# Third output tiles of the last two halves as a Strassen pair, earlier scores for the last half, and packed masks

## The chip, the cores and the metric

One NeuronCore of a Trainium2 chip runs the whole kernel. The metric is device time in microseconds; the kernel before takes 241.64 us, the median of three runs (241.13 to 242.92).

Five engines work side by side, each with a queue of its own that it works off in order: PE (TensorE, matrix products), DVE (VectorE), ACT (ScalarE), POOL (GpSimd) and SP (which here only issues transfers). They wait for each other through semaphores. "PEld" in a profile is PE loading weights.

## The reference

```python
def _attn_ref(q, k, v, n_global, n_local):        # B, H, S, D = 4, 8, 768, 64
    scores = scale * np.matmul(q, k.transpose(0, 1, 3, 2))
    ...
    is_global = pos[None, :] < int(n_global)       # 8 first keys
    is_local = (rel >= 0) & (rel < int(n_local))   # the last 96 keys
    keep = is_global | is_local
    scores = np.where(keep, scores - slopes * dist, -1e9)
    ...                                            # softmax over keys
    return np.matmul(a, v)

def _moe_ref(x, w_gate, w_val, w_out):             # x: 3072 x 512, inner 1536
    gate = np.maximum(x @ w_gate, 0.0)
    val = x @ w_val
    return gate * val @ w_out
```

The output of the attention, with its 8 heads side by side, is the `x` of the gated network. Inputs and output are float32; the kernel multiplies in bfloat16.

## The kernel before

The 3072 rows are cut into eight *halves* (two per batch entry) of 384 rows, each of three tiles of 128 rows. For every half there are two jobs.

*Attention of a half*, cut into 26 small pieces by `attention_pieces`. Heads go in four pairs. For a pair, `pair_scores` makes the scores of two groups of key tiles in four PSUM banks (L397), `pair_exps` takes the exponential (L406, ACT), `masks` multiplies by a mask that holds the distance bias and the zeros (L359, DVE, one multiply per key tile; for odd halves three in the first group and two in the second, for even halves two and two). `piece_av` multiplies by the values (L427) and takes a logarithm (L436) and, once per pair, an exponential of its negative (L441) to get the reciprocal of the sums; `piece_norm` multiplies by it (L446, DVE) and so writes `xT`, the input of the network. The masks lie in `m_all`, made once by `make_mask` from the distances `dd`. Keys and queries of a later half are prepared by `early_pieces`: casts on POOL (L363), transposing transfers in SP's queue (L368), and copies of the keys into their tiles on POOL (`piece_order`, L259 to L265).

*The network of a half*, made by `ffn_pieces`. Twelve chunks of 128 inner columns: `gate` (four matmuls of 384 columns, L518, then a ReLU on ACT, L525) and `val` (four more, then a multiply on DVE that writes the chunk into `ht`, L531). Then the output. Of the three tiles of a half, the third is made plainly by `outp`: twelve matmuls of 512 columns (L538) in four parts, a copy on ACT (L543) and a store (L544). The first two are made together by Strassen's scheme for a 2 x 2 block product: seven products `p1` to `p7` of six matmuls of 256 columns (`block`, L583) in place of eight, with sums of parts of `ht` on the left (`sum_cb`, `sum_ad`, `sum_de`, DVE: L567, L571, L576), sums of parts of the output weights on the right (made once, L809), and additions and copies that put the results together (L599 to L629). Their stores are L593.

PSUM has eight banks: three (`ff`) for the network and five (`x`) for the attention and for the products `p2` and `p5`. The tiles of a pool are reused in turn, so that a new product waits until the one three (or five) before it has been read.

Half 0 and half 1 have a start of their own, and half 2's attention is worked into their end. From `c = 2` on, stage `c` is one turn of this loop, and sets the order of work: the network of half `c` is a list of items, each with a weight, and the pieces of the attention of half `c + 1` and of the preparation of half `c + 2` are laid over it.

```python
def spread(items, first, last):
    n = len(items)
    return [(first + (i + 0.5) / n * (last - first), f) for i, (_, f) in enumerate(items)]
```

`weave` issues the items of the network in order and adds up their weights; a piece is issued as soon as the sum has reached its place times the total weight. The order is fixed when the program is built: each engine's queue holds its instructions in the order in which they are issued here. In a stage the first item is the start of chunk 0 (weight 1.0), then its rest (0.15 and 0.15), then 22 items of 0.65 for the other chunks, then four parts of the third tile and seven products of 0.65 each.

Of the kernel before, what the change touches and what calls it, by code (L numbers as in the profile page):

```python
# [8 lines left out]
FP32 = mybir.dt.float32  # L9
BF16 = mybir.dt.bfloat16  # L10
AF = mybir.ActivationFunctionType
ALU = mybir.AluOpType
# [3 lines left out]
def kernel(  # L16
# [12 lines left out]
    nc = tc.nc  # L29

    B, H, S, D = q.shape
    NG = int(n_global)
    NL = int(n_local)
    DM = H * D
    DFF = moe_w_gate.shape[1]
    N_DC = DM // 128
    N_FC = DFF // 128
    HP = H // 2
    QH = S // 2
    NN = 3  # L40
    KT = 128 - NG
    PK = KT // NN
    WQ = 72
    NHALF = 2 * B
# [8 lines left out]
    for half in range(2):  # L53
        for j in range(NT):
            w0 = PK * j - 128 * half
            a, b_ = max(0, w0), min(128, w0 + WQ)
# [15 lines left out]
    late = {}  # L72
# [21 lines left out]
    wg = [const.tile([128, N_DC, GW * 128], BF16, name=f"wg{i}") for i in range(N_FC // GW)]  # L94
    wv = [const.tile([128, N_DC, GW * 128], BF16, name=f"wv{i}") for i in range(N_FC // GW)]
    wo_sb = const.tile([128, N_FC, DM], BF16)
    dd = const.tile([128, 2, NN, WQ], BF16)
    m_all = const.tile([128, H, 2, NN, WQ], BF16)

    def w_of(t, dc, fc):  # L100
# [70 lines left out]
    vb3 = firstp.tile([128, H, D], BF16, name="vb3")  # L171
    rc0 = [firstp.tile([128, QH], FP32, name=f"rc{p}") for p in range(HP)]
    kq0 = firstp.tile([128, 2, H, NN * D], FP32, name="kq0")
    kq1 = setupp.tile([128, 2, H, NN * D], BF16, name="kq1")

    def rows_of(src, s, h0, h1):
# [150 lines left out]
    def scores(s, p, g):  # L327
# [18 lines left out]
            c += NN * w  # L346
        nc.scalar.activation(es[:, :, 0:cols], ps[:, :, 0:cols], AF.Exp, bias=0.0, scale=scale)  # L347

    def masks(s, p, g, steps=steps_of):
        for j in steps[s % 2][g]:  # L350
            _, a, w, m = by[s % 2, j]
            es, c = es_of[s, p, j]
            for_all = es[:, :, c : c + NN * w]
            mk = m_all[:, 2 * p : 2 * p + 2, 0 if j == 0 else 1, :, m : m + w]
            if w == WQ:
                mk = mk.rearrange("k e n p -> k e (n p)")
            else:
                for_all = for_all.rearrange("k e (n p) -> k e n p", n=NN)
            nc.vector.tensor_mul(for_all, for_all, mk)  # L359
# [133 lines left out]
    def attention_pieces(s):  # L493
        QK = lambda p: [(0.15, lambda g=g: piece_qk(s, p, g)) for g in range(3)]
        AV = lambda p: [(0.29, lambda e=e: piece_av(s, p, e)) for e in range(2)]
        N = lambda p: [(0.0, lambda: piece_norm(s, p))]
        g = QK(3)
        a = AV(2)
        gap = [(0.0, lambda: None)]
        return (QK(0) + QK(1) + AV(0) + N(0) + gap + QK(2) + AV(1) + N(1) + gap  # L500
                + g[0:1] + a[0:1] + g[1:2] + a[1:2] + g[2:3] + N(2) + AV(3) + N(3))
# [4 lines left out]

    begin_of = {}

    def ffn_pieces(c):
        ht = ht_pool.tile([128, N_FC, QH], BF16, name="ht")  # L510
        st = {}
# [38 lines left out]
            if c == 2:  # L550
                product(wg, "g", 1, 0, N_DC - 1)


        N2, D2 = N_FC // 2, DM // 2
        tiles_ = [slice(n * 128, (n + 1) * 128) for n in range(2)]

        def sums_of(name, *shape):
            if name not in st:
                st[name] = late["sums"].tile([128, *shape], BF16, name=name)
            return st[name]  # L560

        cb = lambda: sums_of("cb", N2, 2, 128)
        ad = lambda: sums_of("ad", N2, 128)
        de = lambda: sums_of("de", N_FC, 128)

        def sum_cb(i0, i1):
            nc.vector.tensor_tensor(cb()[:, i0:i1].rearrange("f i n t -> f i (n t)"), ht[:, i0:i1, 0:256],  # L567
                                    ht[:, N2 + i0 : N2 + i1, 0:256], op=ALU.add)

        def sum_ad(i0, i1):  # L570
            nc.vector.tensor_tensor(ad()[:, i0:i1], ht[:, i0:i1, tiles_[0]],  # L571
                                    ht[:, N2 + i0 : N2 + i1, tiles_[1]], op=ALU.add)

        def sum_de(i0, i1):
            x, y = (1, 0) if i0 < N2 else (0, 1)
            nc.vector.tensor_tensor(de()[:, i0:i1], ht[:, i0:i1, tiles_[x]], ht[:, i0:i1, tiles_[y]],  # L576
                                    op=ALU.subtract)

        def block(key, pool, left, right, start, stop):
            if start:  # L580
                st[key] = psum[pool].tile([128, 512], FP32, name=f"{pool}_ps")
            for i in range(N2):
                nc.tensor.matmul(st[key][:, 0:D2], lhsT=left(i), rhs=right(i),  # L583
                                 start=start and i == 0, stop=stop and i == N2 - 1,
                                 skip_group_check=not start)
            return st[key][:, 0:D2]

        c0, c1 = slice(0, D2), slice(D2, DM)
        bs = lambda name: lambda i: late["bs"][name][:, i]
        V2 = nc.vector.tensor_tensor  # L590

        def store(n, cols, eng=nc.sync):
            eng.dma_start(out=out_v[c, n][:, cols], in_=st["r", n][:, cols])  # L593

        def p4():
            for n in range(2):
                st["r", n] = late["osb"].tile([128, DM], FP32, name="osb")
            ps = block("d", "ff", lambda i: ht[:, N2 + i, tiles_[1]], bs("b21-b11"), True, True)
            nc.scalar.copy(st["r", 0][:, c0], ps)  # L599

        def p3():
            ps = block("c", "ff", lambda i: ht[:, i, tiles_[0]], bs("b12-b22"), True, True)
            nc.scalar.copy(st["r", 0][:, c1], ps)

        def p1():
            ps = block("a", "ff", lambda i: ad()[:, i], bs("b11+b22"), True, True)
            nc.scalar.copy(st["r", 1][:, c1], ps)

        def p2():
            ps = block("b", "x", lambda i: cb()[:, i, 1], lambda i: wo_sb[:, i, c0], True, True)  # L610
            V2(st["r", 1][:, c0], ps, st["r", 0][:, c0], op=ALU.add)
            V2(st["r", 1][:, c1], st["r", 1][:, c1], ps, op=ALU.subtract)

        def p5():
            ps = block("e", "x", lambda i: cb()[:, i, 0], lambda i: wo_sb[:, N2 + i, c1], True, True)
            V2(st["r", 0][:, c1], ps, st["r", 0][:, c1], op=ALU.add)
            V2(st["r", 0][:, c0], st["r", 0][:, c0], ps, op=ALU.subtract)
            if c == NHALF - 1:
                store(1, c0)
                store(0, c1)  # L620

        def p6():
            ps = block("c", "ff", lambda i: de()[:, i], bs("b11+b12"), False, True)
            V2(st["r", 1][:, c1], ps, st["r", 1][:, c1], op=ALU.add)
            store(1, slice(0, DM) if c < NHALF - 1 else c1, nc.sync if c < NHALF - 1 else nc.scalar)

        def p7():
            ps = block("a", "ff", lambda i: de()[:, N2 + i], bs("b21+b22"), False, True)
            V2(st["r", 0][:, c0], ps, st["r", 0][:, c0], op=ALU.add)  # L629
            store(0, slice(0, DM) if c < NHALF - 1 else c0)  # L630

        behind = {2: [lambda: sum_de(0, 3)], 5: [lambda: sum_de(3, 6)], 8: [lambda: sum_cb(0, 3)],
                  9: [lambda: sum_ad(0, 3)], 10: [lambda: sum_de(6, 9)]}

        def val_and_sums(fc):
            val(fc)
# [5 lines left out]
        for fc in range(N_FC):  # L642
            f1.append((0.65, lambda fc=fc: gate(fc)))
            f1.append((0.65, lambda fc=fc: (val if c < 1 else val_and_sums)(fc)))
        f2 = [(0.65, lambda n=n, part=part: outp(n, part))
              for n in (range(NN) if c < 1 else (NN - 1,)) for part in range(4)]
        if c >= 2:
            f1[:2] = [(1.0, begin_of[c][0]), (0.15, begin_of[c][1]), (0.15, begin_of[c][2])]
        if c == 2:
            f1[0] = (1.5, f1[0][1])  # L650
            f1[3] = (0.15, lambda: gate(1, N_DC - 1))
        if c >= 1:
            f2 += [(0.65, f) for f in (p4, p3, p1, p2, p5, p6, p7)]
            for at, f in ((5, lambda: sum_de(9, 12)), (3, lambda: sum_cb(3, 6)), (2, lambda: sum_ad(3, 6))):
                f2.insert(at, (0.0, f))
        return f1, f2

# [1 line left out]
# [4 lines that stand above are left out]
# [119 lines left out]
    for f in ("m1 g0 m3 v0 m2 g1 K3 K2 m0 g3 K1 S30 S31 g2 K0 S20 v3 S11 v1 S21 A3 N3 v2 S00 S01 "  # L782
# [10 lines left out]
        else:  # L793
# [3 lines left out]
    early.close()  # L797
    ctx.enter_context(open_psum(ff=3, x=5))
    pool = ctx.enter_context(tc.tile_pool(name="late", bufs=1, reuse_waits="tile"))
    late["osb"] = ctx.enter_context(tc.tile_pool(name="osb", bufs=3, reuse_waits="tile"))  # L800
    late["sums"] = ctx.enter_context(tc.tile_pool(name="sums", bufs=1, reuse_waits="tile"))
    late["bs"] = {name: pool.tile([128, N_FC // 2, DM // 2], BF16, name=f"bs{i}")
                  for i, name in enumerate(("b21-b11", "b12-b22", "b11+b22", "b11+b12", "b21+b22"))}

# [14 lines left out]
    for f in (*casts[:7], lambda: nc.gpsimd.tensor_copy(held, wo_sb[0:1, N_FC - 1, 0:1]),  # L819
# [9 lines left out]
          [(0.33, order_k[2]), (0.38, order_k[3])],  # L829
          pieces, spread(early_pieces(3), 0.58, 0.88),  # L830
          spread([(0.0, lambda name=name, part=part: wo_sum(name, part)) for name in late["bs"] for part in range(2)],
                 0.1, 0.74))

    for c in range(2, NHALF):
        placed = []
        if c + 1 < NHALF:
            placed.append(spread(attention_pieces(c + 1), *((0.07, 0.82) if c == 2 else (0.0, 0.8))))
        if c + 2 < NHALF:
            load_qk(c + 2, 0, H)
            load_v_half(c + 2)  # L840
            placed.append(spread(early_pieces(c + 2), 0.25, 0.75))
        f1, f2 = ffn_pieces(c)
        weave(f1 + f2, *placed)

# [34 lines left out]
```

## Time and profile before

| | |
|---|---|
| runs | 242.92, 241.13, 241.64 us |
| profiled execution | 241.74 us, of which the span from first to last instruction is 239.9 |
| busy, share of the span | PE 97%, DVE 72%, ACT 64%, PEld 61%, POOL 36% |
| PE's granted clock | 0.998 of full speed |
| stage 5, 6, 7 begin at | 159.4, 186.4, 213.85 us |
| L518 (gate and val) | 768 matmuls, 80.7 + 80.2 us busy |
| L538 (plain output tiles) | 112 in the records, 29.6 us busy |
| L583 (Strassen products) | 294 matmuls |

"Busy" is the time in which an engine had an instruction under way. PE's matmuls overlap one another: a group's mean duration is longer than the spacing at which they follow each other, and the spacing is what adds up. The chain that ended last, followed in order of time, shows these spacings. A wait is the idle time of an engine ahead of an instruction, put down to the instruction that released it.

### The profile page before, as it was taken

How to read it: one execution, taken by the hardware profiler on the slowest of the kernel's cores; microseconds unless marked ns; L12 is line 12 of the kernel's file. 1: busy time of each engine (PE TensorE's matmuls, PEld its weight loads, DVE VectorE, ACT ScalarE, POOL GpSimd, SP SyncE). 2: the span in 40 equal slices, each digit the busy share in tenths (PEclk: the TensorE clock that was granted, in tenths of full speed). 3: DMA queues.
4: the chain of work that ended last, by engine and by line, in shares of the span. 5: the costliest groups of instructions: out<-in, count | busy, mean ns of one | idle time of the engine just before them, and what ended most of it. 6: DMA issues, size and time to landing. Idle time of an engine off the chain costs nothing.

```text
span 239.9 us, 5355 instructions
## 1 busy us (share of the span) xinstructions
PE 233.5 (97%) x1937; PEld 146.6 (61%) x1945; DVE 173.3 (72%) x456; ACT 153.4 (64%) x347; POOL 85.9 (36%) x202
## 2 busy tenths in 40 slices
PE   7899999999999999999999999999999999999994
PEld 3655555665458566666668566676658566676663
DVE  7775955869677788777787687866887677764643
ACT  5897883337775777748774777638774677733330
POOL 6767893208414860903274060902350000000000
PEclk9999999999999999999999999999999999999999
DMA  6999999993976997098519939398431200030003
GB/s 200 181 198 177 257 234 219 185 162 61 270 178 134 301 150 131 8 185 257 108 25 122 285 93 133 19 166 262 67 68 44 90 0 0 3 129 3 4 27 104
DMA packets 69603, 31.42 MB, mean 131 GB/s; under 512 B 47160, under 2 KB 66616, under 8 KB 69576
## 3 DMA queue, kind: packets, MB, share of 16 engines
q0 software_dynamic: 31744, 8.71, 35.3%
q1 hardware_dynamic: 36616, 21.45, 35.1%
q10 hardware_dynamic: 1216, 0.92, 1.2%
q8 instruction: 15, 0.25, 0.4%
q14 instruction: 12, 0.10, 0.1%
HBM read 28.41 MB, written 6.29 MB: 145 GB/s over the span
## 4 chain that ended last, share of the span: by engine, by line
PE 91%; ACT 3%; DVE 2%; issue 1%; ACTq 0%
PE ff_ps L518 53%; PE ff_ps L538 9%; PE ff_ps L583 8%; PE x_ps L427 6%; PE x_ps L397 4%; PE x_ps L583 3%; PE t_ps L459 2%; PE s_ps L341 2%; PE t_ps L272 1%; PE t_ps L682 1%; ACT lnd L436 1%; PE t_ps L310 1%; DVE xT L446 1%; PE s_ps L321 1%; ACT rcp L441 0%
## 5 line engine op out<-in xcount | busy, mean ns | idle before, releaser
L518 PE MATMUL ff_ps<-xT,wg 128*128 128x384 bf16 x384 | 80.7, 326 | 0.5 <-ACT grelu L525 0.4
L518 PE MATMUL ff_ps<-xT,wv 128*128 128x384 bf16 x384 | 80.2, 326 | 0.0
L531 DVE TENSOR_TENSOR ht<-ff_ps,grelu 128x384 bf16<-128x384 f32 x96 | 53.1, 554 | 28.5 <-PE ff_ps L518 13.8
L525 ACT ACTIVATE grelu<-ff_ps 128x384 bf16<-128x384 f32 x96 | 47.1, 492 | 39.4 <-PE ff_ps L518 20.9
L518 PEld LDWEIGHTS <-wg 128*128 128x128 bf16 x384 | 35.9, 98 | 23.9 <-issue 0.9
L518 PEld LDWEIGHTS <-wv 128*128 128x128 bf16 x384 | 36.1, 97 | 23.4 <-issue 1.2
L406 ACT ACTIVATE es<-x_ps 128x360 bf16<-128x360 f32 (+2 forms) x96 | 36.8, 444 | 16.9 <-PE x_ps L397 16.8
L359 DVE TENSOR_TENSOR es<-es,m_all 128x432 bf16<-128x432 bf16 (+4 forms) x108 | 31.2, 334 | 8.2 <-ACT es L406 7.8
L446 DVE TENSOR_TENSOR xT<-x_ps,rcp 64x384 bf16<-64x384 f32 x48 | 26.6, 554 | 9.4 <-ACT rcp L441 8.8
L436 ACT ACTIVATE lnd<-x_ps 64x384 f32<-64x384 f32 x48 | 23.3, 485 | 12.5 <-PE x_ps L427 11.8
L538 PE MATMUL ff_ps<-wo_sb,ht 128*128 128x512 bf16 x112 | 29.6, 379 | 0.4
L363 POOL CAST kqc<-ks 128x384 bf16<-128x384 f32 x24 | 11.6, 532 | 32.3 <-DMA ks<-in_k_dram 32.3
L137 POOL DMA_DIRECT2D vbuf<-in_v_dram x25 | 21.6, 880 | 2.6 <-DMA wv<-in_moe_w_val_dram 2.1
L427 PE MATMUL x_ps<-es,vbuf 128*128 128x216 bf16 (+4 forms) x216 | 21.8, 225 | 0.0
L427 PEld LDWEIGHTS <-vbuf 128*128 128x128 bf16 x216 | 15.8, 97 | 7.7
L538 PEld LDWEIGHTS <-ht 128*128 128x128 bf16 x120 | 10.8, 97 | 9.8 <-issue 0.2
L263 POOL COPY kT<-kqT 128x240 bf16<-128x240 bf16 x16 | 6.9, 430 | 23.0 <-DMA kqT<-kqc 20.5
L363 POOL CAST kqc<-qs 128x384 bf16<-128x384 f32 x24 | 11.6, 522 | 8.1 <-DMA qs<-in_q_dram 8.1
L259 POOL COPY kT<-kqT 128x360 bf16<-128x360 bf16 x10 | 6.0, 604 | 19.9 <-DMA kqT<-kqc 19.9
L441 ACT ACTIVATE rcp<-lnd 128x384 f32<-128x384 f32 x24 | 12.6, 524 | 0.7
L347 ACT ACTIVATE ef<-s_ps 128x720 bf16<-128x720 f32 (+2 forms) x16 | 10.9, 710 | 2.1 <-PE s_ps L341 1.8
L397 PE MATMUL x_ps<-kqT,kT 64*128 64x216 bf16 (+4 forms) x216 | 11.8, 224 | 0.2
(115 smaller groups left out, 252.8 us busy)
## 6 DMA issues: line engine op xcount, KB each, us to landing
out_dram<-osb SPq DMA_DIRECT2D x22, 256.0 KB, 2.7
ks<-in_k_dram SPq DMA_DIRECT2D x6, 768.0 KB, 5.5
qs<-in_q_dram SPq DMA_DIRECT2D x6, 768.0 KB, 12.1
vbuf<-in_v_dram POOLq DMA_DIRECT2D x21, 120.0 KB, 7.9
wg<-in_moe_w_gate_dram POOLq DMA_DIRECT2D x3, 512.0 KB, 7.9
wv<-in_moe_w_val_dram POOLq DMA_DIRECT2D x3, 512.0 KB, 9.8
wo_sb<-in_moe_w_out_dram POOLq DMA_DIRECT2D x1, 1536.0 KB, 19.6
kq<-in_q_dram ACTq DMA_DIRECT2D x2, 192.0 KB, 4.7
```

Source lines behind the costliest of these rows:

```text
L137: nc.gpsimd.dma_start(out=v_dst(b, NG + r0, NG + r0 + n, j), in_=v[b, :, KT * j + r0 : KT * j + r0 + n, :].rearrange("h p d -> p h d"))
L359: nc.vector.tensor_mul(for_all, for_all, mk)
L363: nc.gpsimd.tensor_copy(kqc[:, :, i].rearrange("t n (h d) -> t h n d", d=D)[:, 2 * p : 2 * p + 2], of[s][:, 2 * p : 2 * p + 2, :].rearrang ...
L406: nc.scalar.activation(es[:, e, 0:c], banks[e][:, 0:c], AF.Exp, bias=0.0, scale=scale)
L427: nc.tensor.matmul(av3[:, :, a : a + w], lhsT=vb[:, j, z0 : z0 + 128], rhs=es[:, e, c : c + NN * w].rearrange("k (n p) -> k n p", n=NN), s ...
L436: nc.scalar.activation(ln[o0 : o0 + 64], av[d0 : d0 + 64, 0:QH], AF.Ln, bias=0.0, scale=1.0)
L446: nc.vector.tensor_tensor(xT_of[s][r, p, :], av_of[s, p, e][r, 0:QH], av_of[s, p, "r"][r], op=ALU.mult)
L518: nc.tensor.matmul(st[key][:, 0:QH], lhsT=w_of(w, dc, fc), rhs=xT_of[c][:, dc, :], start=(dc == 0), stop=(dc == N_DC - 1))
L525: nc.scalar.activation(gr, psg[:, 0:QH], AF.Relu, bias=0.0, scale=1.0)
L531: nc.vector.tensor_tensor(ht[:, fc, :], psv[:, 0:QH], st["gr", fc], op=ALU.mult)
L538: nc.tensor.matmul(ps2, lhsT=ht[:, fc, n * 128 : (n + 1) * 128], rhs=wo_sb[:, fc, :], start=(fc == 0), stop=(fc == N_FC - 1))
L583: nc.tensor.matmul(st[key][:, 0:D2], lhsT=left(i), rhs=right(i), start=start and i == 0, stop=stop and i == N2 - 1, skip_group_check=not s ...
```

## The change

Three things.

- Halves 6 and 7 (`PAIRED`) no longer make their third tiles plainly. The third tile of half 6 waits for that of half 7, and in stage 7 the two go through a Strassen pair of their own, ahead of the pair of half 7's first two tiles. `strassen` is the old code, made a function of the two tiles; `sum_cb` of the new pair goes one tile at a time, since the two lie in different `ht`. In stage 6 the seven products follow the last `val` at once, with `p3` ahead of `p4` and `p4` in an `x` bank (`bare`). There is a fourth `osb` buffer.
- The first three of the 26 attention pieces of half 7 (the scores, exponentials and masks of its first head pair) are issued in stage 5, at 0.82 to 0.93 of its weight; the other 23 are spread over 0 to 0.74 of stage 6 in place of 0 to 0.8.
- `pack_mask` copies the masks of the first score group on POOL into one tile per kind of half, in the columns' order of the scores; from half 3 on, `masks` multiplies that group by it in one DVE instruction. The copies are laid at 0.7 to 0.9 of the list that ends halves 0 and 1. `dd` moves to a pool that is closed early.

```diff
+    def pack_mask(half, i):
+        todo = [by[half, j] for j in steps_later[half][0]]
+        if half not in packed_of:
+            packed_of[half] = late["packed"].tile([128, H, sum(NN * t[2] for t in todo)], BF16, name=f"packed{half}")
+        c = sum(NN * t[2] for t in todo[:i])
+        j, _, w, m = todo[i]
+        nc.gpsimd.tensor_copy(
+            packed_of[half][:, :, c : c + NN * w].rearrange("k h (n t) -> k h n t", n=NN),
+            m_all[:, :, 0 if j == 0 else 1, :, m : m + w])
...
     def masks(s, p, g, steps=steps_of):
+        if s > 2 and g == 0:
+            mk = packed_of[s % 2][:, 2 * p : 2 * p + 2]
+            es = es_of[s, p, steps[s % 2][0][0]][0][:, :, 0 : mk.shape[2]]
+            nc.vector.tensor_mul(es, es, mk)
+            return
...
+        def sum_cb_of(i):
+            V2(cb()[:, :, i], h(i, 0, N2), h(i, N2, N_FC), op=ALU.add)
...
+        return sum_cb, sum_cb_of, sum_ad, sum_de, [(0.65, f) for f in (((p3, p4) if bare else (p4, p3)) + (p1, p2, p5, p6, p7))]
+
+    PAIRED = (6,)
...
+        plain = range(NN) if c < 1 else () if c - c % 2 in PAIRED else (NN - 1,)
+        sum_cb, _, sum_ad, sum_de, products = strassen([(c, ht, 0), (c, ht, 1)], "sums", c in PAIRED)
         behind = {2: [lambda: sum_de(0, 3)], 5: [lambda: sum_de(3, 6)], 8: [lambda: sum_cb(0, 3)],
                   9: [lambda: sum_ad(0, 3)], 10: [lambda: sum_de(6, 9)]}
+        rest = (lambda: sum_ad(3, 6), lambda: sum_cb(3, 6), lambda: sum_de(9, 12))
+        if c in PAIRED:
+            third_of[c] = ht
+        elif c - 1 in PAIRED:
+            _, cb3, ad3, de3, products3 = strassen([(c, ht, NN - 1), (c - 1, third_of[c - 1], NN - 1)], "sums3")
+            behind[1] = [lambda: cb3(1)]
+            behind[6] = [lambda: ad3(0, N_FC // 2)]
+            behind[7] = [lambda: de3(0, N_FC // 2)]
+            rest = (lambda: cb3(0), lambda: de3(N_FC // 2, N_FC)) + rest
...
-            f2 += [(0.65, f) for f in (p4, p3, p1, p2, p5, p6, p7)]
-            for at, f in ((5, lambda: sum_de(9, 12)), (3, lambda: sum_cb(3, 6)), (2, lambda: sum_ad(3, 6))):
+            f2 += (products3 if c - 1 in PAIRED else []) + products
+            places = (2, 3, 5) if plain else (0, 1, 2) if c in PAIRED else (0, 1, 2, 3, 4)
+            for at, f in list(zip(places, rest))[::-1]:
                 f2.insert(at, (0.0, f))
...
+          spread([(0.0, lambda half=half, i=i: pack_mask(half, i)) for half, i in ((1, 0), (1, 1), (1, 2), (0, 0), (0, 1))],
+                 0.7, 0.9))
+    ahead = {}
     for c in range(2, NHALF):
         placed = []
-        if c + 1 < NHALF:
-            placed.append(spread(attention_pieces(c + 1), *((0.07, 0.82) if c == 2 else (0.0, 0.8))))
...
+        if c + 1 < NHALF:
+            pieces = ahead.pop(c + 1, None) or attention_pieces(c + 1)
+            placed.append(spread(pieces, *(0.07, 0.82) if c == 2 else (0.0, 0.74) if c in PAIRED else (0.0, 0.8)))
+        if c + 1 in PAIRED:
+            ahead[c + 2] = attention_pieces(c + 2)
+            placed.append(spread([ahead[c + 2].pop(0) for _ in range(3)], 0.82, 0.93))
```

## The prediction

> **What bounds the kernel now.** I read the page's busy times and the waits first, then the chain that ended last in order of time, then the timeline where the change lands.
>
> ```profile
> PE 233.5 (97%) x1937; PEld 146.6 (61%) x1945; DVE 173.3 (72%) x456; ACT 153.4 (64%) x347; POOL 85.9 (36%) x202
> PE ff_ps L518 <- ACT grelu L525: 0.4, 1, 0.4
> ```
>
> TensorE (PE) is busy 97% of 239.9 us and its list of waits adds up to 2.3 us, nearly all in the first microseconds. VectorE (DVE), ScalarE (ACT) and GpSimd (POOL) follow it. So only TensorE work that goes, or a wait that comes, moves the time.
>
> ```profile
> 186.38 0.97 PE ff_ps L518 x6
> 187.36 0.41 PE x_ps L397 x10
> 187.77 1.08 PE ff_ps L518 x6
> 188.85 0.02 issue
> 188.87 0.81 PE ff_ps L518 x4
> ...
> 206.06 0.21 PE ff_ps L538
> 206.28 0.05 issue
> 206.33 1.03 PE ff_ps L538 x4
> ...
> 229.45 0.21 PE ff_ps L538
> 229.66 0.05 issue
> 229.72 2.32 PE ff_ps L538 x10
> 232.04 1.97 PE ff_ps L583 x18
> 234.00 1.31 PE x_ps L583 x12
> 235.31 1.32 PE ff_ps L583 x12
> ```
>
> Columns: start, us, work. Stage 6 runs from 186.38, stage 7 from 213.85. L538 is a plain output tile, L583 the seven Strassen products. The 0.02 at 188.85 matters: there `val(1)` starts the moment the ReLU of `gate(0)` has freed its bank.
>
> ```profile
> 187.64 0.79 ACT L406 ACTIVATE es<-x_ps 128x336 bf16<-128x336 f32 x2 [3.47 <-PE x_ps L397]
> 188.32 0.50 ACT L525 ACTIVATE grelu<-ff_ps 128x384 bf16<-128x384 f32 x1
> 188.69 0.85 ACT L406 ACTIVATE es<-x_ps 128x360 bf16<-128x360 f32 x2
> 206.17 0.56 DVE L531 TENSOR_TENSOR ht<-ff_ps,grelu 128x384 bf16<-128x384 f32 x1 [0.78 <-ACT lnd L436]
> ```
>
> The ReLU ends at 188.82, `val(1)` starts at 188.87: no slack. The last `ht` of stage 6 is complete at 206.73, 0.67 after its matmuls (206.06); today 2.6 us of plain tile hide that.
>
> **The change, part by part.**
>
> *Third tiles as a pair.* Removed from the path: stage 6's tile, 0.21 + 0.05 + 1.03 + 0.65 + 0.65 = 2.59 us (its later parts are two rows of 0.65), and stage 7's, 0.21 + 0.05 + 2.32 = 2.58. Added: 7 x 6 = 42 matmuls of 256 columns, and today's 42 in stage 7 take 1.97 + 1.31 + 1.32 = 4.60. So **-0.57 us**, the only work that leaves the path; bounds -0.67 to -0.47 from the rounding of these pieces.
>
> The trace's spacings are 216 ns (0.65 for three) for 512 columns and 109 ns (1.97 for eighteen) for 256. The Trainium skill, page "TensorE: Matmul & The Clock Gate", section "Back-to-back issue gap", speaks against the change: in a stream of weight loads and matmuls it measured about 131 ns for 512 columns and 81 for 128. With some 98 ns for 256 between them (an estimate from that page) 24 matmuls would cost 3.1 us and 42 would cost 4.1, a loss of 1.0. The trace is not like that, and the sum goes by it.
>
> *The sums of the pair, in stage 7.* Five DVE adds of 768 elements, 0.55 each by L567 (0.79 if they went like two L576 of 0.39). Three stand behind `val(1)`, `val(6)`, `val(7)`: eviction 0.55 + sum 0.55 to 0.79 against 1.30 us of matmuls per chunk, the last a little over. Two follow the last `val`; the products then need them later than they are made: the last eviction ends 0.8 after the matmuls, `cb3(0)` at 1.4, `de3` at 1.9, and they are used by the fifth product (2.6) and the seventh (3.9). The second group's `p3` wants the bank of the first group's `p6` at 5.25; DVE frees it at about 4.8. Zero, hidden by DVE's idle 7.3 of 15.6 us; bounds 0 to +0.5. In SP's queue the store of stage 6's tile (210.19) and that of stage 7's (232.69) go; two of 256 KB come, issued over 3 us before the last ones and landing in 2.7, the page's median. Zero; late by 1 us they would still be ahead of the last store.
>
> *Scores of half 7 in stage 5.* The ten matmuls (0.41, and 0.1 that the next group loses) only change stage. They stand between `p3` and `p1`, at about 183.1; their keys are copied by 177.4 (POOL), and their fourth bank is freed by the normalisation, whose first half ends at 182.8. No wait. But DVE must now apply masks between the additions of `p2` and `p5`: packed mask 184.3 to 184.8, `p2` 185.0 to 185.7, second group's masks to 186.2, `p5` to 186.9, `p6` to 187.3 (0.335 per addition, as at 184.51, 184.85, 185.18). `val(0)` of stage 6 wants the bank of `p6` at 187.22: **+0.11**, bounds 0 to +0.3.
>
> *Start of stage 6.* This is what I weigh most. `weave` puts a piece behind the item at which the running weight reaches its place. Now: weight 22.75 (15.6 + 11 x 0.65), 26 pieces over 0.8, hence every 0.70: the first at 0.35, the second at 1.05. The opening item weighs 1.0, so the second (the exponentials of the second score group) falls behind `gate(0)`. After: weight 20.15, 23 pieces over 0.74, every 0.648: at 0.324 and 0.972, both ahead of `gate(0)`. ACT's queue becomes two pairs of exponentials and then the ReLU for which `val(1)` waits, where today the ReLU stands between them. The second pair takes 0.70 (188.69 to the next start at 189.39); PE has no slack here, and behind it stand all its matmuls. **+0.75** (0.70, and part of the ReLU's start behind a late pair). Bounds +0.4 (stage 2's own wait on this line) to +1.0.
>
> *End of stage 6.* With no plain tile, `p3` (0.66) and `p4` follow the last `val` at once. `p4`'s sixth matmul reads the last `ht`, 1.2 us after it. In the built order DVE has the two normalisations of the last head pair right ahead of that `ht`. From the last AV start, 1.6 us before the end of the matmuls: logarithm 0.5 later, reciprocal 0.52 after it, normalisation 0.55 after that (208.15, 208.65, 209.17, 209.72), 1.1 for both, 0.55 for `ht`: 0.5 + 0.52 + 0.55 + 1.1 + 0.55 - 1.6 = 1.6. PE waits 1.6 + 0.05 - 1.2 = **+0.5**. Bounds 0 (if the head pair's chain ran early) to +0.9. Its sums (`ad` 0.35, `cb` 0.55) then arrive just ahead of `p1` and `p2`. The stage as a whole is no fuller: from 186.38 to 206.06 ACT is busy 15.4 of 19.7 us, loses the first pair's exponentials (0.68 + 0.70 and their tails) and gains the last pair's logarithms and reciprocal (0.97 + 0.52).
>
> *`dd` in another pool, a fourth `osb` buffer.* Space only: its last reader, `make_mask(0)`, is done by 21.4 us (L239), long before the late pools open. Zero, unless a late tile waited for it, which no row shows.
>
> *Packed masks.* Per head pair of an odd half three multiplies (0.65 together) become one of 672 elements, by 768 in 0.55 and 432 in 0.39 some 0.50; of an even half two (0.48) become one of 480, 0.41. That is 12 x 0.15 + 8 x 0.07 = 2.4 us of DVE. No wait of PE on a mask shows in stages 2 to 7, so it is worth 0; bounds -0.1 to +1.6 (the slower rival). The five POOL copies: L259 (360 in 0.60) and L265 (48 in 0.24) give 0.18 us + 1.17 ns per element, so 2.2 twice, 0.86, 0.63, 0.41: 6.3 us. The first 2.2 delays the last cast of half 3, which ends at 67.06; the transposes start at 69.33 anyway, behind a store in SP's queue. The second delays key orders of head pairs 2 and 3 from 77.06 on, needed at 87.98, and the loads of values; the casts behind those wait for input until 83.72 and 87.52. Twice as long would still fit (first keys 78.6, wanted 79.19). Zero.
>
> Two masks took 1.26 us at 84.17 beside POOL casts, and 0.60 at 189.58 with POOL idle. The skill's page "SBUF — State Buffer", section "Who interferes with whom", has a VectorE operation with two SBUF inputs and a GpSimd one that reads SBUF exclude each other for a whole instruction. By that rule a mask could lose a whole 2.2 us copy twice, where the row shows 0.66; next use of what DVE makes there is at 69.92, so perhaps +0.5 by the rule.
>
> **Sum.** -0.57 + 0.11 + 0.75 + 0.5 = +0.79 us. The profiled execution took 241.74 (span 239.9 and 1.8 around it), so 242.5; it lies 0.10 above the median of 241.64, hence **242.4 us**. One per cent, 2.4 us, is about what a measurement of this kernel can tell from no change, and this is a third of it.
>
> **Rivals.**
> 1. *The saving arrives whole.* The three waits don't come, because queues drain faster than I add up. For it: PE shows no idle in any later stage. Against: 188.85, where slack is zero. 241.64 - 0.57 = 241.1.
> 2. *The packed multiply is slow and DVE holds the path* (slower than before). If it ran at the rate of L531 (384 in 0.55), 672 elements would take 0.97 in place of 0.65. The last head pair of a half has next to no margin: masks at 206.65 to 207.24, AV at 207.19. With 0.32 on each of 5 halves +1.6, and the waits above: 244.0. It decides from about 0.8 us per multiply on. Against it: all bf16 adds from SBUF run at 0.55 for 768.
> 3. *The change doesn't do what it says*: the early scores stall stage 5. Should their fourth bank wait for the second half of the normalisation as well (0.56 of L446), they and all behind them are 0.6 late: 243.0. Against: the first half ends 0.5 before it is wanted, the keys are there 5 us before.
>
> **How the numbers follow.** Forecast 0.58 (242.0 to 243.0 its own range), rival 1 0.28, rival 2 0.06, rival 3 0.08. The range 240.9 to 243.2 takes in rival 1 with its rounding and rival 3, and leaves out rival 2 and the sum of all upper bounds. Faster by over 1% would need 2.4 us of TensorE work gone, and 0.57 is all there is: 0.02. Slower by over 1% comes from rival 2 and part of the tail of the waits: 0.08. Within 1%: 0.90.
>
> **What would show it.** Right: a wait of PE on the ReLU of some 0.7 us near the second chunk of stage 6, one on `ht` of some 0.5 at its end, 84 products of 109 ns in stage 7, and PE's busy time down by about 0.6. Wrong: no such waits and a span near 239.4 (rival 1), packed multiplies over 0.8 us (rival 2), or a PE wait of over 0.5 at the scores in stage 5 (rival 3).

## The result, and the profile after

The changed kernel takes **243.21 us** (median, 242.75 to 244.08) where the kernel before takes 241.68 on the same chip: 1.0065 times as long, 95% interval 1.0049 to 1.0081. That is +1.5 us where +0.79 was forecast, and 0.01 us above the range. The interval reaches 0.16% to either side; the prediction had taken some 1% for what can be told from no change. Its profiled execution took 243.21 too, with a span of 241.4 (before: 239.9). In the program lines L518 is now L636, L538 is L656, L583 is L570, L397 is L415, L406 is L424, L446 is L464, L525 is L643, L531 is L649, L359 is L377, L809 is L862, and the sums L567, L571 and L576 are L553, L560 and L564; L366 is the packed multiply and L358 the packing copy.

The busy times of the page after, and one of its groups:

```profile
PE 233.3 (97%) x1957; PEld 148.4 (61%) x1963; DVE 176.0 (73%) x435; ACT 153.4 (64%) x348; POOL 90.9 (38%) x207
L366 DVE TENSOR_TENSOR es<-es,packed 128x672 bf16<-128x672 bf16 (+1 forms) x20 | 9.8, 492 | 6.8 <-ACT es L424 6.6
```

TensorE's busy time hardly moves (-0.2, where the prediction gave some -0.6 as a sign). The packed multiply takes 0.49 us in the mean: rival 2 is out. What came is waits. From the list of waits of after (total, times, longest):

```profile
PE ff_ps L636 <- ACT grelu L643: 1.2, 2, 0.7
PE x_ps L415 <- DVE xT L464: 0.8, 1, 0.8
PE x_ps L570 <- DVE ht L649: 0.5, 1, 0.5
```

Before, the list held of these only the ReLU's 0.4. It stands at 19.52 us, in the start of half 0, in both kernels; the prediction took it for one of stage 2 and set a bound by it. The first and the third are the two that the prediction named; the timeline of after has them where it put them:

```profile
188.70 1.52 ACT L424 ACTIVATE es<-x_ps 128x336 bf16<-128x336 f32 x4 [2.96 <-PE x_ps L415]
190.08 0.91 ACT L643 ACTIVATE grelu<-ff_ps 128x384 bf16<-128x384 f32 x2
190.65 0.81 PE L636 MATMUL ff_ps<-xT,wv 128*128 128x384 bf16 x4 [0.75 <-ACT grelu L643]
...
208.01 1.14 DVE L464 TENSOR_TENSOR xT<-x_ps,rcp 64x384 bf16<-64x384 f32 x2
209.18 0.56 DVE L649 TENSOR_TENSOR ht<-ff_ps,grelu 128x384 bf16<-128x384 f32 x1
209.80 0.28 PE L570 MATMUL x_ps<-bs,ht 128*128 128x256 bf16 x1 [0.47 <-DVE ht L649]
```

ACT works through four exponentials and only then the ReLU that `val(1)` waits for: 0.75, forecast 0.75. DVE works through two normalisations and only then the last `ht`: 0.47, forecast 0.5. The forecast wait of `val(0)`, too short for the list, is the gap between the first two matmuls of `gate(0)` and those of `val(0)`, 0.54 where 0.32 is the spacing of the same rows before (186.22 and 186.54):

```profile
187.06 0.49 PE L636 MATMUL ff_ps<-xT,wg 128*128 128x384 bf16 x2
187.60 0.48 PE L636 MATMUL ff_ps<-xT,wv 128*128 128x384 bf16 x2
```

The second of the three waits above stands at 69 us, in the work that ends halves 0 and 1, where nothing was forecast. The timeline of before:

```profile
66.21 1.00 DVE L359 TENSOR_TENSOR es<-es,m_all 128x432 bf16<-128x432 bf16 x2 [0.62 <-ACT es L406]
67.14 0.54 DVE L809 TENSOR_TENSOR bs<-wo_sb 128x768 bf16<-128x768 bf16 x1
68.42 1.14 DVE L446 TENSOR_TENSOR xT<-x_ps,rcp 64x384 bf16<-64x384 f32 x2 [0.73 <-ACT rcp L441]
68.54 0.79 PE L397 MATMUL x_ps<-kqT,kT 64*128 64x216 bf16 x8
```

and of after:

```profile
66.11 2.13 DVE L377 TENSOR_TENSOR es<-es,m_all 128x432 bf16<-128x432 bf16 x2 [0.61 <-ACT es L424]
66.31 1.77 POOL L358 COPY packed<-m_all 128x1728 bf16<-128x1728 bf16 x1
68.17 0.85 DVE L862 TENSOR_TENSOR bs<-wo_sb 128x768 bf16<-128x768 bf16 x1
69.04 1.14 DVE L464 TENSOR_TENSOR xT<-x_ps,rcp 64x384 bf16<-64x384 f32 x2
69.65 0.31 PE L415 MATMUL x_ps<-kqT,kT 64*128 64x216 bf16 x3 [0.83 <-DVE xT L464]
```

Two mask multiplies that took 1.00 take 2.13 beside a packing copy. They and a weight sum (L862) stand ahead of the normalisation in DVE's queue, the normalisation starts at 69.04 in place of 68.42, and the scores wait for the bank that its first half frees. Before, the eight scores followed one another in 0.79, where eight of 216 columns need some 0.4 (an estimate: in stage 6 ten take 0.48). They too met that normalisation, without an idle entry, and the chain that ended last shows it:

```profile
68.42 0.56 DVE xT L446
69.02 0.31 PE x_ps L397 x2
```

There was no slack there.

The starts of the stages by the chain that ended last:

| | stage 3 | stage 4 | stage 5 | products of stage 5 | stage 7 | last product ends |
|---|---|---|---|---|---|---|
| before | 104.78 | 131.69 | 159.36 | 181.80 | 213.85 | 236.63 |
| after | 105.40 | 132.31 | 159.78 | 182.12 | 213.35 | 238.13 |
| after - before | +0.62 | +0.62 | +0.42 | +0.32 | -0.50 | +1.50 |

The 0.62 of the copy is there at stage 3. From there to stage 5's products after takes 76.72 and before 77.02; the nine kernels below whose chain shows that stretch take 76.7 to 77.2 for it, with packing and without, so the 0.30 regained is put down to differences between executions. From those products to the end it is 56.01 against 54.83: +1.18, where the four terms of the sum said +0.79.

### The profile page after: what moved, and what is told of

Its sections match the earlier page's. It is cut to its first block, busy times and chain, and to the rows that moved or that the text cites. A ratio compares the mean times of both kernels' runs of the same rounds, so it can differ in the third digit from the quotient of the medians.

```text
span 241.4 us, 5385 instructions
## 1 busy us (share of the span) xinstructions
PE 233.3 (97%) x1957; PEld 148.4 (61%) x1963; DVE 176.0 (73%) x435; ACT 153.4 (64%) x348; POOL 90.9 (38%) x207
## 4 chain that ended last, share of the span: by engine, by line
PE 86%; DVE 6%; ACT 4%; issue 2%; DVEq 0%; ACTq 0%
PE ff_ps L636 51%; PE ff_ps L570 8%; PE ff_ps L656 6%; PE x_ps L445 5%; PE x_ps L415 4%; PE x_ps L570 4%; PE t_ps L477 2%; PE s_ps L341 2%; DVE xT L464 2%; PE t_ps L272 1%; PE t_ps L733 1%; PE t_ps L310 1%; DVE es L377 1%; ACT lnd L454 1%; ACT es L424 1%
## 5 line engine op out<-in xcount | busy, mean ns | idle before, releaser
L636 PE MATMUL ff_ps<-xT,wg 128*128 128x384 bf16 x384 | 80.7, 326 | 0.5 <-ACT grelu L643 0.4
L636 PE MATMUL ff_ps<-xT,wv 128*128 128x384 bf16 x384 | 80.2, 326 | 0.8 <-ACT grelu L643 0.7
L649 DVE TENSOR_TENSOR ht<-ff_ps,grelu 128x384 bf16<-128x384 f32 x96 | 53.2, 555 | 29.8 <-PE ff_ps L636 14.3
L643 ACT ACTIVATE grelu<-ff_ps 128x384 bf16<-128x384 f32 x96 | 47.0, 492 | 39.1 <-PE ff_ps L636 19.4
L636 PEld LDWEIGHTS <-wv 128*128 128x128 bf16 x384 | 36.1, 98 | 24.4 <-issue 2.2
L636 PEld LDWEIGHTS <-wg 128*128 128x128 bf16 x384 | 35.9, 98 | 23.5 <-issue 0.9
L424 ACT ACTIVATE es<-x_ps 128x360 bf16<-128x360 f32 (+2 forms) x96 | 36.6, 444 | 16.4 <-PE x_ps L415 16.3
L464 DVE TENSOR_TENSOR xT<-x_ps,rcp 64x384 bf16<-64x384 f32 x48 | 26.6, 554 | 8.2 <-ACT rcp L459 7.5
L656 PE MATMUL ff_ps<-wo_sb,ht 128*128 128x512 bf16 x90 | 23.9, 379 | 0.3
L377 DVE TENSOR_TENSOR es<-es,m_all 128x432 bf16<-128x432 bf16 (+4 forms) x56 | 19.6, 390 | 1.9 <-ACT es L424 1.7
L366 DVE TENSOR_TENSOR es<-es,packed 128x672 bf16<-128x672 bf16 (+1 forms) x20 | 9.8, 492 | 6.8 <-ACT es L424 6.6
L656 PEld LDWEIGHTS <-ht 128*128 128x128 bf16 x96 | 8.6, 97 | 7.4
L415 PE MATMUL x_ps<-kqT,kT 64*128 64x216 bf16 (+4 forms) x216 | 12.0, 224 | 0.9 <-DVE xT L464 0.8
```

What stands on the lines that cost most here:

```text
L415: nc.tensor.matmul(banks[e][:, c : c + NN * w].rearrange("k (n t) -> k n t", n=NN), lhsT=kt[r, j, :], rhs=qd[r, :, a : a + w], start=True, ...
L424: nc.scalar.activation(es[:, e, 0:c], banks[e][:, 0:c], AF.Exp, bias=0.0, scale=scale)
L464: nc.vector.tensor_tensor(xT_of[s][r, p, :], av_of[s, p, e][r, 0:QH], av_of[s, p, "r"][r], op=ALU.mult)
L636: nc.tensor.matmul(st[key][:, 0:QH], lhsT=w_of(w, dc, fc), rhs=xT_of[c][:, dc, :], start=(dc == 0), stop=(dc == N_DC - 1))
L643: nc.scalar.activation(gr, psg[:, 0:QH], AF.Relu, bias=0.0, scale=1.0)
L649: nc.vector.tensor_tensor(ht[:, fc, :], psv[:, 0:QH], st["gr", fc], op=ALU.mult)
```

## Experiments

The reading above is theory A: the packing costs some 0.6 where its first copy runs beside DVE, and the rest is three waits, on `p6`'s bank, on the ReLU and on `ht`, all met in stage 6, so that each can be taken away by itself. The rivals have other letters, each named where it first stands. Kernels are compared by the ratio to the kernel before as recorded with the runs (1.0065 for the change; it can differ by some 0.001 from the quotient of the medians); its median was 241.71 for the first four, 241.43 for the next four and 241.38 for the last four. Each kernel has one profiled execution. Where profiles are compared, two stretches tell where time went: from stage 5's products to the last product's end (*late stretch*: before 54.83, after 56.01), and from one normalisation to the next around the first copy (*normalisation step*: before 63.16 to 68.42, 5.26; after 63.05 to 69.04, 5.99).

**No packing, the rest of the change kept.**

```diff
-        if s > 2 and g == 0:
+        if False:
...
-          spread([(0.0, lambda half=half, i=i: pack_mask(half, i)) for half, i in ((1, 0), (1, 1), (1, 2), (0, 0), (0, 1))],
-                 0.7, 0.9))
```

> The changed kernel without packing: no copies on POOL, and masks multiplied one key tile at a time as before. Theory A (the loss is four waits of PE, the first of them 0.62 us at 69.6 us because a 1.77 us packing copy on POOL holds up a mask multiply on DVE): that wait goes, and what packed masks save later (0.3 us, read as the shift between the two traces from stage 4 to stage 6) is lost too, so 0.3 us below the changed kernel, about 242.9, and the scores at 69 us start as early as before. Rival B (the wait there has another cause, such as other addresses of tiles, and the copies are hidden): 243.2 to 243.5 and the wait stays.

242.54, ratio 1.0037 (1.0024 to 1.0049). The normalisation step is 5.26 again and the scores' wait at 69 us is gone; the two waits of stage 6 stay:

```profile
PE ff_ps L636 <- ACT grelu L643: 1.2, 2, 0.7
PE x_ps L570 <- DVE ht L649: 0.5, 1, 0.5
PE x_ps L415 <- DVE xT L464: 0.2, 1, 0.2
```

The 0.2 is another wait, at 88.29: there the sum `de` (L564) took 0.57 beside POOL casts, 0.36 before, and put a normalisation off. Without packing 0.28% less time, 0.7 us: more than twice the 0.3 that A said, since A took the 0.30 regained after stage 3 for the masks' doing. B, by which the wait stays, falls. The late stretch is 56.02, as in the change.

**Pieces of stage 6 over 0 to 0.78.** The first two places move to 0.34 and 1.03, so the second exponentials fall behind `gate(0)` again.

```diff
-            ... (0.0, 0.74) if c in PAIRED else (0.0, 0.8)))
+            ... (0.0, 0.78) if c in PAIRED else (0.0, 0.8)))
```

> The changed kernel with the 23 pieces of stage 6 spread over 0 to 0.78 in place of 0 to 0.74, so that the second group's exponentials fall behind the first gate, and the last normalisation behind the last val. Theory A: the 0.75 us wait on the ReLU goes; the 0.47 us wait of the second product on the last ht goes too but comes back on the third product, whose sum now stands behind the normalisation (0.4). About 242.5. Rival C (ScalarE's work has to be done somewhere in a stage that is too full, so a wait taken away comes back at the next ReLU): 243.0 to 243.2.

243.09, ratio 1.0059 (1.0041 to 1.0078): next to nothing gained, where A said 242.5; the time is rival C's. The waits:

```profile
PE x_ps L415 <- DVE xT L464: 0.9, 1, 0.9
PE ff_ps L570 <- DVE ad L560: 0.6, 1, 0.6
PE ff_ps L636 <- ACT grelu L643: 0.4, 1, 0.4
```

The ReLU's 0.7 is gone (the 0.4 is that of half 0's start), and with it `ht`'s; but at the end of the stage `p1` now waits 0.6 on the sum `ad`, which the later pieces push back in DVE's queue. Half of the 1.2 is lost one step further on, not at the next ReLU as C has it. By the timelines the late stretch is 55.70 against 56.17, so the profile shows 0.47 gained; why the median of five runs doesn't is open.

**Only the ReLU's wait.** All places of stage 6 a hair later (first two at 0.41 and 1.05 in place of 0.32 and 0.97), so that the end of the stage stays as it is.

```diff
-            ... (0.0, 0.74) if c in PAIRED else (0.0, 0.8)))
+            ... (0.004, 0.744) if c in PAIRED else (0.0, 0.8)))
```

> The changed kernel with the pieces of stage 6 shifted by 0.004 of its weight, which only moves the second group's exponentials behind the first gate. Theory A: the wait of 0.75 us on the ReLU goes and nothing else, 242.45; the wait on the last ht at the end of stage 6 stays at 0.4 to 0.5. Rival C: 243.0 to 243.2.

242.86, ratio 1.0052 (1.0034 to 1.0069): 0.3 less than the change where 0.7 was expected, and under C's 243.0. The profile shows the whole of it where it was put: from stage 5's products to stage 7's start 30.51 in place of 31.23, with no ReLU wait in stage 6 and `ht`'s 0.5 still there. The rest is put down to scatter, which isn't shown: this profiled execution was 0.62 behind the change's at stage 3 already, before any line that differs.

**Both ends of stage 6.** Places over 0 to 0.8, and the three sums of the pair ahead of its products in place of among them.

```diff
-            places = (2, 3, 5) if plain else (0, 1, 2) if c in PAIRED else (0, 1, 2, 3, 4)
+            places = (2, 3, 5) if plain else (0, 0, 0) if c in PAIRED else (0, 1, 2, 3, 4)
...
-            ... (0.0, 0.74) if c in PAIRED else (0.0, 0.8)))
+            ... (0.0, 0.8)))
```

> The changed kernel with the pieces of stage 6 spread over 0 to 0.8 and the three sums of its pair put together ahead of the first product, so that on DVE the last ht and the sums stand ahead of the last normalisation. Theory A: both the wait on the ReLU (0.75) and that on the last ht (0.47) go, 242.0. Rival C: 243.0 or more, with waits elsewhere in stage 6.

241.81, ratio 1.0001 (0.9987 to 1.0015). The waits of stage 6 on the ReLU, on `ht` and on the sums are all gone:

```profile
PE x_ps L415 <- DVE xT L464: 1.3, 2, 1.0
PE ff_ps L636 <- ACT grelu L643: 0.4, 1, 0.4
```

The late stretch is 54.46, 1.55 shorter than the change's and 0.37 shorter than before: the pair's -0.57 and what is left of one wait, 0.2 of `val(0)` on the bank of `p6`. With the early collision still in it (1.0 of the scores' 1.3 stands at 69.28), the kernel is level with the one before. C, which said 243.0 or more, falls.

**Packing alone.** The kernel before with `pack_mask`, its five copies, the packed multiply and `dd` in the other pool; no pair and no early scores.

```diff
+        if s > 2 and g == 0:
+            mk = packed_of[s % 2][:, 2 * p : 2 * p + 2]
...
+          spread([(0.0, lambda half=half, i=i: pack_mask(half, i)) for half, i in ((1, 0), (1, 1), (1, 2), (0, 0), (0, 1))],
+                 0.7, 0.9))
```

> The kernel before with the packed masks alone (the five copies on POOL and one multiply for the first score group); third tiles, pieces and order of halves 6 and 7 as before. Theory A: the mask multiply that meets the 1.77 us copy is held up and PE loses 0.6 us at 69 us, of which shorter masks give back at most 0.1 to 0.3 later: 242.1 to 242.3. Rival D (the packed masks pay for themselves, by less work on VectorE in every stage): 241.4 to 241.7.

242.41, ratio 1.0029 (1.0005 to 1.0053): slower, so D falls. The loss is A's, 0.7 us (1.0 by the medians), but its profile doesn't show A's place: the copy came later (67.74), the masks at 66.48 took 0.94, the normalisation step is 5.26, and a later pair of masks took 1.24 beside the next copies. Which DVE instruction a copy meets differs from profile to profile: in "only the ReLU's wait", whose order of work is the change's up to stage 6, the masks took 1.08 and the weight sum behind them 1.97.

**The pair alone.** No packing, no early scores; all 26 pieces over 0 to 0.8.

```diff
-        if s > 2 and g == 0:
+        if False:
...
-          spread([(0.0, lambda half=half, i=i: pack_mask(half, i)) for half, i in ((1, 0), (1, 1), (1, 2), (0, 0), (0, 1))],
-                 0.7, 0.9))
...
-            ... (0.0, 0.74) if c in PAIRED else (0.0, 0.8)))
-        if c + 1 in PAIRED:
+            ... (0.0, 0.8)))
+        if False:
```

> The Strassen pair of the third tiles alone: no packed masks, and all 26 pieces of the last half's attention in stage 6, over 0 to 0.8. Theory A: 0.57 us of matmuls saved; the second group's exponentials again fall ahead of the first gate (places 0.31 and 0.93), 0.75 lost on the ReLU; the sums of the pair stand around the last normalisation on VectorE, 0.4 to 0.6 lost at the end of stage 6: 242.3. Rival C (stage 6 without the tile is too short for 26 pieces, so that ScalarE holds PE throughout): over 243.

242.22, ratio 1.0028 (1.0004 to 1.0052), as A expects; C said over 243. The pair by itself loses time too:

```profile
PE ff_ps L636 <- ACT grelu L643: 1.2, 2, 0.7
PE x_ps L570 <- DVE cb L553: 0.7, 1, 0.7
```

Both waits belong to the shorter stage 6: with 2.6 us of plain tile gone the pieces stand denser, and the products meet the stage's last DVE work. The early scores are not what makes them, nor is the packing.

**Packing with its copies elsewhere.** As "both ends", and the three copies for odd halves at 43 to 46 us, where POOL otherwise waits for a transfer.

```diff
+    for f in (*casts[:7], *(lambda i=i: pack_mask(1, i) for i in range(3)),
...
-          spread([(0.0, lambda half=half, i=i: pack_mask(half, i)) for half, i in ((1, 0), (1, 1), (1, 2), (0, 0), (0, 1))],
-                 0.7, 0.9))
+          spread([(0.0, lambda half=half, i=i: pack_mask(half, i)) for half, i in ((0, 0), (0, 1))],
+                 0.82, 0.9))
```

> Both ends of stage 6 mended as in the run with 0 to 0.8 and the sums first, and the three packing copies for odd halves moved to some 42 to 47 us, where POOL waits for weights and VectorE only reads PSUM and one tile from SBUF. Theory A: the 0.6 us at 69 us goes too, 241.2, under the kernel before; the copies put off the last cast there by up to 1 us, and the scores that follow from it are at 57 us, with about 1 us to spare. Rival: the delay of that cast reaches PE and gives the 0.6 us back, 241.8.

241.80, ratio 1.0016 (0.9986 to 1.0046): a miss of A's 241.2, and the figure of the rival that was put beside it. At 66 us the mechanism did what was expected (masks at 66.28 took 1.05, normalisation step 5.26), but the median didn't fall by the 0.6, and the profile has the 0.6 again before stage 3 (105.42, where the change has 105.40). The rival's place, a late cast for the scores at 57 us, isn't it. The sum `de` at 87.51 met POOL casts, took 0.93 in place of 0.36 and put off a normalisation for which the scores wait:

```profile
86.37 1.86 POOL L381 CAST kqc<-qs 128x384 bf16<-128x384 f32 x4
87.51 0.93 DVE L564 TENSOR_TENSOR de<-ht 128x384 bf16<-128x384 bf16 x1
88.96 0.33 PE L415 MATMUL x_ps<-kqT,kT 64*128 64x192 bf16 x3 [0.51 <-DVE xT L464]
```

That is the change's collision once more, with a cast for the copy. The same sum took 0.57 without any packing, so whether the packing brings this one on isn't shown. The runs lie between 240.95 and 244.23, so the interval excludes little.

**Copies in slices.** Each 1728-element copy as four of 432.

```diff
-        nc.gpsimd.tensor_copy(
-            packed_of[half][:, :, c : c + NN * w]...
+        step = 2 if w == WQ else H
+        for h in range(0, H, step):
+            nc.gpsimd.tensor_copy(
+                packed_of[half][:, h : h + step, c : c + NN * w]...
```

> The changed kernel with each packing copy of 1728 elements made as four of 432, one per head pair, 0.15 us more per copy in sum. If a VectorE operation with two SBUF inputs waits for the whole POOL copy that is under way, it now waits for at most 0.6 us, and then takes its turn: the first mask multiply beside them takes 0.7 to 1.1 us in place of 2.1, and PE's wait at 69 us shrinks from 0.83 to 0.3 to 0.5: 242.8. Rival: both only share bandwidth, so the same bytes hold it up as long: 2.1 and 243.2.

242.78, ratio 1.0068 (1.0042 to 1.0093): no better than whole copies (1.0065). The 242.8 of the expectation is met in microseconds only; the kernel before, too, was faster in these runs (241.43). The profiled execution can't be compared: TensorE waited 1.4 us for a weight transfer (L638 on `wv`; lines here stand two further on) in it, and the copies met other instructions (normalisation step 5.26). Slicing doesn't help; why not is open.

**The copies alone, read by nobody.** The change with the five copies where they are, and the masks multiplied by step.

```diff
-        if s > 2 and g == 0:
+        if False:
```

> The changed kernel with the five packing copies left where they are and nothing reading them: the masks are multiplied by step as before. Theory A (the copy itself, beside a DVE instruction with two inputs in SBUF, is the cost): the two masks at 66 us still take over 1.5 us and the scores at 69 us still wait over 0.5; 243.2 to 243.4. Theory E (the cost lies in the packed tile being read or waited for): masks at 1.0, 242.5.

243.83 (four runs), ratio 1.0112 (1.0097 to 1.0127): slower than the change itself and than A's 243.2 to 243.4. E, with 242.5, falls. The timeline shows another victim:

```profile
65.45 0.96 DVE L377 TENSOR_TENSOR es<-es,m_all 128x432 bf16<-128x432 bf16 x2 [0.94 <-ACT es L424]
66.20 1.70 POOL L358 COPY packed<-m_all 128x1728 bf16<-128x1728 bf16 x1
66.34 1.97 DVE L862 TENSOR_TENSOR bs<-wo_sb 128x768 bf16<-128x768 bf16 x1
68.34 1.14 DVE L464 TENSOR_TENSOR xT<-x_ps,rcp 64x384 bf16<-64x384 f32 x2
68.94 0.31 PE L415 MATMUL x_ps<-kqT,kT 64*128 64x216 bf16 x3 [0.79 <-DVE xT L464]
```

Here the masks were done (0.96, not over 1.5 as expected) and the weight sum, 0.54 before, took 1.97. The normalisation step is 5.95 and the scores wait 0.79, as in the change; the late stretch is 56.02. So it is the copy, whether it meets the masks or the sum. With the no-packing kernel at 1.0037, the copies cost 0.75% and the packed multiply gives 0.47% back; both figures rest on these four runs, and the profile, the fastest of the four, doesn't show what is lost beyond the change.

**Both ends, no packing.**

```diff
-        if s > 2 and g == 0:
+        if False:
...
-          spread([(0.0, lambda half=half, i=i: pack_mask(half, i)) for half, i in ((1, 0), (1, 1), (1, 2), (0, 0), (0, 1))],
-                 0.7, 0.9))
...
+            places = (2, 3, 5) if plain else (0, 0, 0) if c in PAIRED else (0, 1, 2, 3, 4)
...
+            ... (0.0, 0.8)))
```

> The pair with its three sums ahead of it and the last half's pieces over 0 to 0.8 of stage 6 (as in the run with both waits taken out, 241.81), but with no packing: the masks of the first score group are multiplied by step, as before. Theory A (the packing's collision at 66 to 69 us costs some 0.6 and its one multiply gives 0.1 to 0.2 back): 241.3 to 241.5, and the wait of the scores (PE L415) on DVE xT at 69 us at most 0.3. Theory D (the packing costs nothing outside the noise): 241.8.

241.02, ratio **0.9985** (0.9972 to 0.9997): faster than before by 0.15%, and 0.3 under A's figure; D falls again. The list of waits has no wait of the scores; the late stretch is 54.46, as with packing.

**The same with two early pieces.** The masks of the second score group stay in stage 6.

```diff
-            placed.append(spread([ahead[c + 2].pop(0) for _ in range(3)], 0.82, 0.93))
+            placed.append(spread([ahead[c + 2].pop(0) for _ in range(2)], 0.82, 0.893))
```

> As the run beside it without packing, with only two pieces of the last half moved into stage 5 instead of three (the masks of the second score group are then not ahead of val(0) on DVE). By the theory the 0.21 us wait of val(0) at 187.4 us goes too: 241.1 to 241.3, that is 0.2 to 0.5 below the kernel before. If the saving of the pair's products (0.57 in the prediction's sum) is eaten elsewhere: 241.5 or more.

240.95, ratio **0.9982** (0.9972 to 0.9992), the lowest of all, though its interval overlaps that of the kernel above, and a little under the expectation. Its timeline at the start of stage 6, and its chain at the end of the stage:

```profile
186.69 0.49 PE L636 MATMUL ff_ps<-xT,wg 128*128 128x384 bf16 x2
187.01 0.49 PE L636 MATMUL ff_ps<-xT,wv 128*128 128x384 bf16 x2
```

```profile
206.45 0.66 PE ff_ps L570 x6
207.10 0.69 PE x_ps L570 x6
207.79 0.52 PE ff_ps L570 x5
```

`val(0)` follows `gate(0)` after 0.32; in the change it followed after 0.54. The products of the pair stand back to back. The late stretch is 54.33, 0.50 shorter than before: the pair's -0.57 arrives, but for 0.07.

**Two early pieces, and packing with its copies moved.**

```diff
+    for f in (*casts[:7], *(lambda i=i: pack_mask(1, i) for i in range(3)),
...
+            placed.append(spread([ahead[c + 2].pop(0) for _ in range(2)], 0.82, 0.893))
```

> Both waits of stage 6 taken out, the three copies for the odd halves moved to 42 to 47 us, and only two pieces of the last half moved into stage 5. By theory A 0.2 below the run with three pieces moved (241.8): 241.6; and level with the run that has no packing (241.1 to 241.3) plus up to 0.3, since the copies of the even half remain.

241.58, ratio 1.0008 (0.9993 to 1.0022), the time that was expected. Late stretch 54.33 and normalisation step 5.26, both as without packing, and stage 3 at 104.82 against 104.88; yet the median is 0.6 higher. What the packing costs here hardly shows in the profiled execution (240.96, the second fastest of twelve; the scores wait 0.20 at 88.37 behind a `de` of 0.61) and stays open. Packing has paid in no version that was run.

## Why the prediction was wrong

Right were the direction, the pair's saving and the three waits of stage 6 that were forecast. By its terms:

| term | forecast | after | shown by |
|---|---|---|---|
| pair's products | -0.57 | -0.50 or a little more | late stretch of the best version |
| `val(0)` on the bank of `p6` | +0.11 | +0.21 | gone with two early pieces: late stretch -0.13 |
| `val(1)` on the ReLU | +0.75 | +0.75 | gone with the hair's shift: stage 6 -0.72 |
| last `ht` | +0.5 | +0.47 | gone with "both ends" |
| packed masks, POOL copies | 0 | +0.62 in the profile, +0.7 in the medians | packing alone, packing taken away |
| not in the sum | | some +0.3 | below |

**The step that failed** is "*Packed masks* ... Zero": the copies were priced by what they delay in POOL's queue, and what they hold up in DVE's was left out of the sum. Two links of it. The first: "No wait of PE on a mask shows in stages 2 to 7, so it is worth 0". A mask delays what stands behind it in DVE's queue, here a weight sum and a normalisation, and it was the normalisation that PE waited for; no list of waits on masks can show that. The second: "next use of what DVE makes there is at 69.92". The next use was the bank of the scores at 68.54. The group's 0.79 for eight matmuls, where ten of them take 0.48 in stage 6, said that they already waited there.

The price stood in the prediction, beside the sum: two masks in 1.26 beside POOL casts against 0.60, that is +0.66, and "perhaps +0.5 by the rule". With the first the sum is +1.45 and the time 243.1. That either comes near is luck. In the profiles the two masks lost 1.13 (2.13 against 1.00) and the weight sum 0.31 (0.85 against 0.54), together 1.44; of this DVE had 0.73 to spare, its idle time ahead of the normalisation before, and 0.71 came through, as the normalisation step shows (5.99 against 5.26). The prediction reckoned neither with the second instruction nor with the slack.

That this one place is the whole price of packing isn't shown: with the copies moved away from it the medians stayed 0.6 to 0.8 above those without packing.

The Trainium skill, page "SBUF — State Buffer", section "Who interferes with whom", says that a VectorE operation with two SBUF inputs and a GpSimd one that reads SBUF exclude each other for a whole instruction. The runs agree but for some 0.15 us. Of the two masks of after the second was the one held up (the trace's durations of that line, shortest, median, longest):

```profile
L377 DVE TENSOR_TENSOR es<-es,m_all x2: 486/1104/1722, 66.1 to 66.5; 128x432 bf16<-128x432 bf16 x1, 128x288 bf16<-128x288 bf16 x1
```

It began at 66.5, after the copy, and ended at 68.24, 0.16 after the copy's end (66.31 + 1.77 = 68.08). Alone a mask of 288 columns takes 0.33 in the mean of before. In the run with unread copies the weight sum, 0.54 before, ended at 68.31, 0.41 after its copy (67.90). Neither got far while the copy ran.

*What was not in the sum.* Late stretch +1.18, and -0.57 + 0.21 + 0.75 + 0.47 makes +0.86. Of the other 0.32 some 0.2 is one group of scores at 194.61: ten matmuls in 0.67 where their neighbours take 0.48, beside the normalisation at 194.35 that frees their bank. The pieces stand denser in 0.74 of a shorter stage. Some 0.1 is not placed. With the places over 0 to 0.8 and the sums first all of it is gone.

*The rivals.* 1, the saving whole: not as built, but it is what the best version does (240.95; the rival said 241.1). 2, a slow packed multiply: 0.49 us against the 0.8 at which it would decide. 3, early scores that stall stage 5: ten scores at 183.43 in 0.41, no wait.

## What to carry to other kernels

Price a moved or added instruction by its whole queue: whatever stands behind it on its engine is late by its worst duration, and the wait then appears on something else. A stage that loses TensorE work loses cover as well: the queues that were hidden by it must be re-spread, or the saving comes back as waits at both ends. A gap need not show as idle time: compare a group's duration with the same group elsewhere before calling a stretch free.

## What the runs showed of the hardware

A GpSimd copy of 1728 bf16 elements per partition takes 1.63 us beside operations with a PSUM input (76.78 in after) and makes one VectorE operation with two SBUF inputs wait nearly to its end: two masks 2.13 to 2.30 in place of 0.91 to 1.18 (three profiles), one sum of 768 elements 1.97 in place of 0.54 to 0.85 (two profiles). POOL casts of 384 elements do it too: a sum of 384 took up to 0.93 in place of 0.36. Operations with a PSUM input were not slowed: `ht` took 0.56 beside the copies at 43 us, and 0.56 elsewhere. Which operation is hit differs from profile to profile, as the masks wait for ACT and the copy stands in POOL's queue behind casts that wait for a transfer; the median shows the cost (0.7 us for packing alone) even where the one profile doesn't.
